# Two attention decodes on one core: moving the softmax steps of the sliding-window half, and loading the output weights in longer rows

## Chip, cores, metric

One core of one Trainium2 chip. The metric is device time of the core in microseconds; most executions of one kernel agree within 0.3%.

## The reference, cut

```python
# A: 4 batches, 32 query heads on 8 key heads, the last W = 2048 of 8192 keys
# B: 4 batches, 32 query heads on 32 key heads, all 8192 keys
q = (x @ wq).reshape(B, 1, 32, 128).transpose(0, 2, 1, 3)
scores = einsum("bhqd,bhkd->bhqk", q, k) * 128 ** -0.5
o = einsum("bhqk,bhkd->bhqd", softmax(scores), v)
out = o.transpose(...).reshape(B, 1, 4096) @ wo         # wo: 4096 x 512
# A's and B's results side by side, all tensors bf16
```

B's caches alone are 537 MB, A's part that is used 34 MB, the four weights 17 MB. Every byte is read once.

## The kernel before

The program works through chunks: 8 of A (one key head, all four batches: 2 MB of keys, 2 MB of values, 512 KB of output weights), then 64 of B (two heads of one batch: 4 MB of keys, 4 MB of values; every four chunks 256 KB of output weights). PE is TensorE, DVE VectorE, ACT ScalarE. One engine, SP (SyncE), issues all loads in order; each waits until PE has freed its buffer. PE transposes keys in groups of 8 tiles of 128, DVE or ACT copies each group out of PSUM (where PE's results land), PE makes scores from it two groups later. Values of chunk c-1 are multiplied between the keys of c and of c+1.

```python
def dma_wo(g):                              # A's output weights: 512 rows of 1 KB
    src = A_wo[g * 4 * P:(g + 1) * 4 * P, :].rearrange("(hl d) n -> d hl n", d=P)
    ... waits=[("fin", g - 2)] ...          # the slot is free when chunk g-2 has its output product

# in emit_T: who copies group g of transposed keys
if (g % 3 == 2) if c >= NCA else (g % 2 == 1):   # ACT, else DVE

def keys_part(c):
    for g in range(ch["NG"]):               # 8 groups in A, 16 in B
        emit_T(ch["s"] + g)
        if g >= SLAG: emit_S(ch["s"] + g - SLAG)
        if 1 <= c < NCA and g == 2: stats_gmax(c - 1)
        if 1 <= c < NCA and g == 3: stats_exp(c - 1)   # bias, shift, exponent, masked spread, sums
        if 2 <= c < NCA and g == 4: emit_fin(c - 2)    # output product
        if 1 <= c < NCA and g == 6: norm_sum(c - 1)
        ...

def values_part(c, nxt):                    # values of c, last scores of nxt
    todo = {2: lambda: emit_S(late[0]), 5: lambda: scores_last(nxt)}
    ...

# after the last pair of chunks
norm_sum(NC - 1)
for g in range(chunks[NC - 1]["NG"]): emit_pv(NC - 1, g)
pv_done(NC - 1); emit_fin(NC - 1)

# PE's instructions are written as two loops, over pairs of chunks of A and of B; the code
# between them (A's serial end) is straight. Both loop heads stand at slot 0 of a block of 256.
sch.emit_looped("pe", e, sems, loop_on(mybir.EngineType.PE, (0, 0)))
```

## Time and profile before

| | before |
|---|---|
| time, median of 3 runs | 1379.57 us (1378.76 to 1380.17) |
| span of the profiled run | 1378.8 us |
| DMA | 587.5 MB, 426 GB/s over the span, plateau 431 to 433 |
| PE busy | 86%, VectorE 47%, ScalarE 32% |

The page splits the span into 40 slices of 34.5 us. The kernel is bound by the DMA: the way to read it is to ask in which slices it moves less than the plateau, and what the issuing queue waited for there. The prediction shows those lines.

### The profile page before, as it was taken

How to read it: one execution, taken by the hardware profiler on the slowest of the kernel's cores; microseconds unless marked ns; L12 is line 12 of the kernel's file. 1: busy time of each engine (PE TensorE's matmuls, PEld its weight loads, DVE VectorE, ACT ScalarE, POOL GpSimd, SP SyncE). 2: the span in 40 equal slices, each digit the busy share in tenths (PEclk: the TensorE clock that was granted, in tenths of full speed). 3: DMA queues.
4: the chain of work that ended last, by engine and by line, in shares of the span. 5: the costliest groups of instructions: out<-in, count | busy, mean ns of one | idle time of the engine just before them, and what ended most of it. 6: DMA issues, size and time to landing. Idle time of an engine off the chain costs nothing.

```text
span 1378.8 us, 59410 instructions
## 1 busy us (share of the span) xinstructions
PE 1179.3 (86%) x26901; PEld 1134.8 (82%) x26901; DVE 641.3 (47%) x1337; ACT 436.0 (32%) x649; POOL 4.8 (0%) x18
## 2 busy tenths in 40 slices
PE   4888799898889888888898888888888898888988
PEld 4776799887879888888898788888888888888887
DVE  1664355454444444444454444444444444444443
ACT  1553234232323322323333223332332233223322
POOL 1000000000000000000000000000000000000000
PEclk9898999999999999999999999999999999999999
DMA  9999999999999999999999999999999999999998
GB/s 401 414 417 416 394 429 432 429 432 433 428 432 433 427 433 432 430 432 432 429 432 433 433 428 433 431 430 432 430 431 433 433 428 432 433 429 432 430 428 356
DMA packets 30373, 587.53 MB, mean 426 GB/s; under 512 B 2816, under 2 KB 11024, under 8 KB 11408
## 3 DMA queue, kind: packets, MB, share of 16 engines
q1 hardware_dynamic: 30328, 587.22, 99.7%
q8 instruction: 16, 0.26, 0.1%
q14 instruction: 5, 0.04, 0.0%
q10 hardware_dynamic: 24, 0.01, 0.0%
HBM read 587.21 MB, written 0.01 MB: 426 GB/s over the span
## 4 chain that ended last, share of the span: by engine, by line
DMA 58%; PE 37%; DVE 2%; issue 1%; SPq 1%; ACT 0%; DVEq 0%
DMA kv<-in_B_k_cache_dram 54%; PE tr L382 22%; PE sc L384 10%; PE po L384 3%; DMA kv<-in_B_v_cache_dram 2%; PE fin L384 2%; DMA kv<-in_B_wq_dram 2%; DVE sA L501 1%; PE ms L384 1%; SPq L339 1%; DVE kt L452 0%; DVE sA L499 0%; ACT pba L564 0%; PE ms L382 0%; DVE rm L510 0%
## 5 line engine op out<-in xcount | busy, mean ns | idle before, releaser
L382 PE MATMUL tr<-identb,kv 128*128 128x128 bf16 x8704 | 703.9, 232 | 155.4 <-DMA kv<-in_B_k_cache_dram 152.2
L452 DVE COPY kt<-tr 128x1024 bf16<-128x1024 bf16 x736 | 503.2, 691 | 466.6 <-PE tr L382 465.3
L382 PEld LDWEIGHTS tr<-identb,kv 128*128 128x128 bf16 x8704 | 559.4, 105 | 181.2 <-DMA kv<-in_B_k_cache_dram 97.0
L450 ACT ACTIVATE kt<-tr 128x1024 bf16<-128x1024 bf16 x352 | 360.0, 1023 | 625.9 <-PE tr L382 625.5
L384 PE MATMUL sc<-qb,kt 128*128 128x64 bf16 x8704 | 447.7, 196 | 9.8 <-DVE kt L452 9.5
L384 PEld LDWEIGHTS sc<-qb,kt 128*128 128x128 bf16 x8704 | 369.7, 100 | 13.8 <-DVE kt L452 11.1
L384 PE MATMUL po<-pbb,kv 128*128 128x64 bf16 x8320 | 294.5, 192 | 8.7 <-issue 6.8
L384 PEld LDWEIGHTS po<-pbb,kv 128*128 128x128 bf16 x8320 | 267.3, 97 | 11.0 <-issue 7.0
L549 ACT ACTIVATE pbb<-sc,negb 64x128 bf16<-64x128 f32 x128 | 51.0, 399 | 297.8 <-DVE negb L539 297.0
L515 DVE TENSOR_REDUCE rm<-sc 64x1 f32<-64x128 f32 x128 | 36.9, 289 | 95.0 <-PE sc L384 94.1
L527 DVE TENSOR_REDUCE gm<-ms 1x2 f32<-1x128 f32 (+1 forms) x72 | 20.1, 279 | 44.9 <-PE ms L382 44.8
L539 DVE COPY negb<-ms 128x1 f32<-128x1 f32 (+1 forms) x72 | 11.4, 158 | 57.1 <-PE ms L384 57.1
L384 PE MATMUL ms<-identf,gx 1*128 1x1 f32 (+1 forms) x144 | 27.8, 260 | 0.0
L384 PEld LDWEIGHTS ms<-identf,gx 1*128 1x128 f32 (+1 forms) x144 | 21.7, 188 | 4.9 <-issue 0.9
L549 ACT ACTIVATION_READ_ACCUMULATOR pbb<-sc,negb 64x1 f32 x128 | 23.7, 185 | 0.0
L382 PE MATMUL ms<-identf,rm 128*1 128x128 f32 (+1 forms) x72 | 19.7, 274 | 2.3 <-DVE rm L510 2.3
L384 PE MATMUL po<-pba,kv 128*128 128x64 bf16 x512 | 20.1, 199 | 0.5 <-ACT pba L564 0.5
L384 PE MATMUL fin<-wos,oz 128*4 128x512 bf16 x66 | 19.6, 378 | 0.3 <-DVE oz L629 0.3
L384 PEld LDWEIGHTS po<-pba,kv 128*128 128x128 bf16 x512 | 17.9, 102 | 0.6 <-ACT pba L564 0.6
L531 DVE TENSOR_SCALAR gx<-gm 1x128 f32<-1x128 f32 (+1 forms) x72 | 15.9, 221 | 2.7 <-DVE gm L527 0.2
L384 PE MATMUL ms<-xT,kv 128*128 128x4 bf16 x256 | 7.1, 166 | 9.1 <-DMA kv<-in_A_wq_dram 4.6
L384 PEld LDWEIGHTS ms<-xT,kv 128*128 128x128 bf16 x256 | 7.0, 104 | 9.3 <-DMA kv<-in_A_wq_dram 4.7
(46 smaller groups left out, 139.5 us busy)
## 6 DMA issues: line engine op xcount, KB each, us to landing
kv<-in_B_k_cache_dram SPq DMA_DIRECT2D x63, 4096.0 KB, 27.3
kv<-in_B_v_cache_dram SPq DMA_DIRECT2D x63, 4096.0 KB, 32.0
kv<-in_A_k_cache_dram SPq DMA_DIRECT2D x8, 2048.0 KB, 12.6
kv<-in_A_v_cache_dram SPq DMA_DIRECT2D x8, 2048.0 KB, 14.2
kv<-in_A_wq_dram SPq DMA_DIRECT2D x1, 4096.0 KB, 12.2
kv<-in_B_wq_dram SPq DMA_DIRECT2D x1, 4096.0 KB, 27.2
wor<-in_A_wo_dram SPq DMA_DIRECT2D x8, 512.0 KB, 8.5
wos<-in_B_wo_dram SPq DMA_DIRECT2D x16, 256.0 KB, 20.8
```

The source lines that it names most:

```text
L339: sch.add_dma("sp", lambda e, x=x: e.dma_start(dst[:, x], src[:, x]), "d_vl%d" % i, waits=waits, key=("vl", j0))
L382: sch.add("pe", lambda e: e.transpose(o, l, r), waits, key)
L384: sch.add("pe", lambda e: e.matmul(o, l, r, start=start, stop=stop), waits, key)
L450: sch.add("act", lambda e: e.activation(dst, src, ACTF.Copy), waits=waits, key=("ev", s))
L452: sch.add("dve", lambda e: e.tensor_copy(dst, src), waits=waits, key=("ev", s))
L501: emit = lambda e, src=src, b=b: e.scalar_tensor_tensor(out=t, in0=src, scalar=mk[:, b:b + 1], in1=t, op0=ALU.mult, op1=ALU.add)
L515: sch.add("dve", lambda e, src=src, pp=pp: e.tensor_reduce(out=rm[pp, m, 0:1], in_=src, axis=AX.X, op=ALU.max), waits=[("S", ch["s_last"]) ...
L527: sch.add("dve", lambda e: e.tensor_reduce(out=gm[0:C, m, 0:U], in_=src, axis=AX.X, op=ALU.max), waits=[("trm", c)], key=("gmax", c))
L531: sch.add("dve", lambda e: e.tensor_scalar(out=dst, in0=gv, scalar1=-scale, scalar2=None, op0=ALU.mult), waits=[("gmax", c)], key=("gx", c))
L539: sch.add("dve", lambda e: e.tensor_copy(negb[:, m, 0:C], ms[:, col:col + C]), waits=[("bc", c)], key=("negb", c))
L549: sch.add("act", lambda e, src=src, pp=pp, n=n, u=u: e.activation(pbv[pp, :, u], src, ACTF.Exp, bias=negb[pp, m, 0:1], scale=scale, accum_ ...
```

## The change

Its intent: in A, take the score work on DVE out of the way of the key copies, so that PE keeps up with the DMA; and load both output weights in rows of 4 KB (A) and 2 KB (B) instead of 1 KB. A longer row puts neighbouring weight rows on one partition, so the head outputs have to be permuted to match: small matmuls with 0/1 matrices ("selection") and copies. For the last chunk the weights are permuted instead (`emit_wol`).

```diff
-            src = A_wo[...].rearrange("(hl d) n -> d hl n", d=P)
+            src = A_wo[...].rearrange("(p r) n -> p (r n)", r=4)
-            src = B_wo[...].rearrange("(hl d) n -> d hl n", d=P)
+            src = B_wo[...].rearrange("(p r) n -> p (r n)", r=2)
-            if (g % 3 == 2) if c >= NCA else (g % 2 == 1):
+            if (g % 3 == 2) if c >= NCA else (g in (0, 1, 3, 5)):
+        def emit_sel(c):                    # 4 (A) or 2 (B) small matmuls, as many DVE copies
+            ...
+        def emit_wol():                     # 4 matmuls of 512 columns, one ACT and one DVE copy
+            ...
+        A_ORDER = {1: ['gmax-1'], 2: ['bc-1', 'shift-1'], 3: ['exp-1'], 5: ['sums-1', 'sel-2'],
+                   6: ['spread-1'], 7: ['norm-1', 'fin-2']}     # key group: step and chunk back
-            todo = {2: lambda: emit_S(late[0]), 5: lambda: scores_last(nxt)}
+            todo = {... the same for B ...} or {0: lambda: emit_S(late[0]), 1: lambda: scores_last(nxt)}   # A
+                if c >= NCA and c % 2 == 1 and g == 8:
+                    emit_sel(ahead(c, 2))
         norm_sum(NC - 1)
+        emit_wol()
         for g in range(chunks[NC - 1]["NG"]):
             emit_pv(NC - 1, g)
```

More of the change, by code (lines that the diff above doesn't have):

```diff
@@ L25 @@
 TRM0, BC0, L0, Q0, XT0 = 0, 256, 288, 320, 448
+Z0 = Q0
 class _Record:
@@ L240, in bass_concat_heads__sliding_block_cached__mha_block_cached__decode_kernel @@
         outsb = sb("outsb", [36, DO], BF16)
+        sel4 = sb("sel4", [P, 4, P], BF16)
+        sel2 = sb("sel2", [P, 2, P], BF16)
+        back2 = sb("back2", [P, 2, 2, P], BF16)
+        zA = sb("zA", [P, 2, 16], BF16)
+        zB = sb("zB", [P, 8], BF16)
+        wol = sb("wol", [P, 2, DO], BF16)
         tr = ps("tr", [P, NTRB, TG * P], BF16)
@@ L274, in bass_concat_heads__sliding_block_cached__mha_block_cached__decode_kernel @@
         sch.add("pool", lambda e: e.memset(pbt[1][:, :, :], 0.0), key=("c_pb", 1))
+        for r in range(4):
+            sch.add("pool", lambda e, r=r: e.affine_select(
+                out=sel4[:, r, :], in_=onesb[:, :], pattern=[[0, 4], [-4, 32]], compare_op=ALU.is_equal,
+                fill=0.0, base=-r, channel_multiplier=1), waits=["c_onesb"])
+        for r in range(2):
+            sch.add("pool", lambda e, r=r: e.affine_select(
+                out=sel2[:, r, :], in_=onesb[:, :], pattern=[[0, 2], [-2, 64]], compare_op=ALU.is_equal,
+                fill=0.0, base=-r, channel_multiplier=1))
+            for u in range(2):
+                sch.add("pool", lambda e, r=r, u=u: e.affine_select(
+                    out=back2[:, u, r, :], in_=onesb[:, :], pattern=[[1, P]], compare_op=ALU.is_equal,
+                    fill=0.0, base=P * u - r, channel_multiplier=-2), key="c_sel" if r == u == 1 else None)
         half_of = {}
@@ L304, in dma_wo @@
         def dma_wo(g):
-            src = A_wo[g * 4 * P:(g + 1) * 4 * P, :].rearrange("(hl d) n -> d hl n", d=P)
+            src = A_wo[g * 4 * P:(g + 1) * 4 * P, :].rearrange("(p r) n -> p (r n)", r=4)
             slot = wo_slot(g)
-            dst = wor[:, slot, :].rearrange("p (hl n) -> p hl n", hl=4)
+            dst = wor[:, slot, :]
             sch.add_dma("sp", lambda e: e.dma_start(dst, src), "d_wo%d" % slot,
@@ L311, in dma_wos @@
         def dma_wos(hp):
-            src = B_wo[2 * hp * P:2 * (hp + 1) * P, :].rearrange("(hl d) n -> d hl n", d=P)
-            sch.add_dma("sp", lambda e: e.dma_start(wos[:, :, :], src), "d_wos",
+            src = B_wo[2 * hp * P:2 * (hp + 1) * P, :].rearrange("(p r) n -> p (r n)", r=2)
+            sch.add_dma("sp", lambda e: e.dma_start(wos[:, :, :].rearrange("p r n -> p (r n)"), src), "d_wos",
                         waits=[("fin", NCA + 4 * hp - 1)] if hp else [], key=("wos", hp))
@@ L532, in stats_gmax, with stats_bc @@
                     waits=[("gmax", c)], key=("gx", c))
-        def stats_exp(c):
-            ch = chunks[c]
-            ab, m, C, U = ch["ab"], c % NSM, ch["C"], ch["U"]
+        def stats_bc(c):
+            m, C = c % NSM, chunks[c]["C"]
             col = BC0 + (c % 2) * 16
@@ L540, in stats_exp, with probs_of @@
             ms_read[:] = [("negb", c)]
-            i = c % NPB
-            prev = c - NPB
-            pw = [("c_pb", ab)] + ([("pv", prev)] if prev >= (0 if ab == 0 else NCA) else [("pv", NONE)] if prev == NCA - 1 else [])
-            pbv = pbt[ab][:, i, 0:ch["NT"] * ch["UC"]].rearrange("p (j x) -> p j x", x=ch["UC"])
-            if ab == 1:
-                for u, pp in HALVES:
-                    src = sc[pp, c % 2, 0:NTB * 2].rearrange("p (j u) -> p u j", u=2)[:, u, :]
-                    n = 2 * ((c - NCA) % 2) + u
-                    sch.add("act", lambda e, src=src, pp=pp, n=n, u=u: e.activation(
-                        pbv[pp, :, u], src, ACTF.Exp, bias=negb[pp, m, 0:1], scale=scale, accum_out=rst[1][pp, n:n + 1]),
-                        waits=[("negb", c), "c_rs"] + rs_read[NSM] + pw, key=("exp", c) if u == 1 else None)
-                sc_read[c % 2] = [("exp", c)]
-                sch.tk[("rs", c)] = sch.tk[("exp", c)]
-                return
+        def probs_of(c):
+            ch = chunks[c]
+            return pbt[ch["ab"]][:, c % NPB, 0:ch["NT"] * ch["UC"]].rearrange("p (j x) -> p j x", x=ch["UC"])
@@ new lines, in exp_B @@
+        def exp_B(c):
+            m, prev = c % NSM, c - NPB
+            pw = [("c_pb", 1)] + ([("pv", prev)] if prev >= NCA else [("pv", NONE)] if prev == NCA - 1 else [])
+            for u, pp in HALVES:
+                src = sc[pp, c % 2, 0:NTB * 2].rearrange("p (j u) -> p u j", u=2)[:, u, :]
+                n = 2 * ((c - NCA) % 2) + u
+                sch.add("act", lambda e, src=src, pp=pp, n=n, u=u: e.activation(
+                    probs_of(c)[pp, :, u], src, ACTF.Exp, bias=negb[pp, m, 0:1], scale=scale, accum_out=rst[1][pp, n:n + 1]),
+                    waits=[("negb", c), "c_rs"] + rs_read[NSM] + pw, key=("exp", c) if u == 1 else None)
+            sc_read[c % 2] = [("exp", c)]
+            sch.tk[("rs", c)] = sch.tk[("exp", c)]
@@ L555, in stats_exp, with shift_A, exp_A @@
+        def shift_A(c):
+            C = chunks[c]["C"]
             t = sA[:, c % 2, :].rearrange("p (j c) -> p j c", c=C)
-            bias = bcast(negb[:, m, 0:C], [[0, NTA], [1, C]])
+            bias = bcast(negb[:, c % NSM, 0:C], [[0, NTA], [1, C]])
             sch.add("dve", lambda e: e.scalar_tensor_tensor(out=t, in0=t, scalar=scale, in1=bias, op0=ALU.mult, op1=ALU.add),
                     waits=[("negb", c)], key=("shift", c))
-            ev = eA[:, c % 2, :]
-            sch.add("act", lambda e: e.activation(ev, sA[:, c % 2, :], ACTF.Exp),
+        def exp_A(c):
+            sch.add("act", lambda e: e.activation(eA[:, c % 2, :], sA[:, c % 2, :], ACTF.Exp),
@@ L562, in stats_exp, with spread_A @@
                     waits=[("shift", c)] + ([("exp", c - 2), ("rs4", c - 2)] if c >= 2 else []), key=("exp1", c))
-            for b in range(NB):
+        def spread_A(c, bs):
+            for b in bs:
                 sch.add("act", lambda e, b=b: e.activation(
-                    pbv.rearrange("p j (b c) -> p j b c", b=NB)[:, :, b, :], ev.rearrange("p (j c) -> p j c", c=C),
+                    probs_of(c).rearrange("p j (b c) -> p j b c", b=NB)[:, :, b, :], eA[:, c % 2, :].rearrange("p (j c) -> p j c", c=REP),
@@ L566, in stats_exp, with sums_A @@
                     ACTF.Copy, scale=mk[:, b:b + 1]),
-                    waits=[("exp1", c), "mk"] + pw if b == 0 else [], key=("exp", c) if b == NB - 1 else None)
-            sch.add("dve", lambda e: e.tensor_reduce(out=rs4[:, m, :], in_=ev.rearrange("p (j c) -> p c j", c=C), axis=AX.X, op=ALU.add),
+                    waits=[("exp1", c), "mk", ("c_pb", 0)] + ([("pv", c - NPB)] if c >= NPB else []) if b == 0 else [],
+                    key=("exp", c) if b == NB - 1 else None)
+        def sums_A(c):
+            m = c % NSM
+            sch.add("dve", lambda e: e.tensor_reduce(out=rs4[:, m, :], in_=eA[:, c % 2, :].rearrange("p (j c) -> p c j", c=REP), axis=AX.X, op=ALU.add),
@@ L569, in stats_exp @@
                     waits=[("exp1", c)], key=("rs4", c))
             sch.add("dve", lambda e: e.tensor_tensor(
-                out=rst[0][:, m, :].rearrange("p (b c) -> p b c", b=NB), in0=bcast(rs4[:, m, :], [[0, NB], [1, C]]),
-                in1=bcast(mk[:, :], [[1, NB], [0, C]]), op=ALU.mult),
+                out=rst[0][:, m, :].rearrange("p (b c) -> p b c", b=NB), in0=bcast(rs4[:, m, :], [[0, NB], [1, REP]]),
+                in1=bcast(mk[:, :], [[1, NB], [0, REP]]), op=ALU.mult),
                 waits=[("rs4", c)], key=("rs", c))
@@ L627, in norm_out @@
                 i1 = rz[:, :].rearrange("p (x y) -> p x y", x=2)
-            waits = [("rinv" if 0 <= c < NCA else "rz", c), ("pv", c)] + ([("fin", c - 2 if c != NCA + 1 else NONE)] if c >= 2 else [])
+            waits = [("rinv" if 0 <= c < NCA else "rz", c), ("pv", c)] + ([("sm", c - 2 if c != NCA + 1 else NONE)] if c >= 2 else [])
             sch.add("dve", lambda e: e.tensor_tensor(out=o, in0=i0, in1=i1, op=ALU.mult), waits=waits, key=("oT", c))
             po_read[:] = [("oT", c)]
+        def emit_sel(c):
+            if 0 <= c < NCA:
+                sel, x, n, z, k = sel4, oT[:, c % NSM, :], 16, zA[:, c % 2, :], 4
+                free = [("fin", c - 2)] if c >= 2 else []
+            else:
+                sel, x, n, z, k = sel2, oz[:, :], 8, zB[:, :], 2
+                free = [("fin", c - 2 if c - 2 >= NCA else NONE)] if c != NONE else []
+            for r in range(k):
+                pe_mm(ms[:, Z0 + r * n:Z0 + (r + 1) * n], sel[:, r, :], x,
+                      waits=[("oT", c)] + ms_read if r == 0 else [], key=("sm", c) if r == k - 1 else None)
+            for h in range(k):
+                pp = slice(h * P // k, (h + 1) * P // k)
+                src = ms[pp, Z0:Z0 + k * n].rearrange("p (r b h) -> p h r b", r=k, b=NB)[:, h]
+                sch.add("dve", lambda e, src=src, pp=pp: e.tensor_copy(z[pp, :].rearrange("p (r b) -> p r b", r=k), src),
+                        waits=[("sm", c)] + free if h == 0 else [], key=("z", c) if h == k - 1 else None)
+            ms_read[:] = [("z", c)]
+        def emit_wol():
+            for u in range(2):
+                o = tr[:, u, :].bitcast(F32)
+                for r in range(2):
+                    pe_mm(o, back2[:, u, r, :], wos[:, r, :], start=r == 0, stop=r == 1,
+                          waits=[("wos2", NC - 1)] if u == r == 0 else [], key=("back", u) if r else None)
+                if u == 0:
+                    sch.add("act", lambda e, o=o: e.activation(wol[:, 0, :], o, ACTF.Copy), waits=[("back", 0)], key=("wol", 0))
+                else:
+                    sch.add("dve", lambda e, o=o: e.tensor_copy(wol[:, 1, :], o), waits=[("back", 1)], key=("wol", 1))
         def emit_fin(c):
@@ L634, in emit_fin @@
             p0 = 0 if ab == 1 else 32
-            if ab == 1:
+            if c == NC - 1:
                 ov = oz[:, :].rearrange("p (b u) -> p b u", u=2)
-                ops = [(ov[:, :, u], wos[:, u, :]) for u in range(2)]
-                waits = [("oT", c), ("wos2", c)]
-            else:
-                w = wor[:, wo_slot(c), :].rearrange("p (hl n) -> p hl n", hl=4)
-                ov = oT[:, c % NSM, :].rearrange("p (u c) -> p u c", c=REP)
-                ops = [(ov[:, :, cc], w[:, cc, :]) for cc in range(REP)]
-                waits = [("oT", c), ("wo", c)]
+                ops = [(ov[:, :, u], wol[:, u, :]) for u in range(2)]
+                waits = [("oT", c), ("wol", 0), ("wol", 1)]
+            elif ab == 1:
+                ops = [(zB[:, r * NB:(r + 1) * NB], wos[:, r, :]) for r in range(2)]
+                waits = [("z", c), ("wos2", c)]
+            else:
+                w = wor[:, wo_slot(c), :].rearrange("p (r n) -> p r n", r=4)
+                ops = [(zA[:, c % 2, r * NB:(r + 1) * NB], w[:, r, :]) for r in range(4)]
+                waits = [("z", c), ("wo", c)]
             lastc = NC - 1 if ab == 1 else NCA - 1
@@ L657, in pv_done, with do_A @@
                 norm_out(c)
+        A_ORDER = {1: ['gmax-1'], 2: ['bc-1', 'shift-1'], 3: ['exp-1'], 5: ['sums-1', 'sel-2'], 6: ['spread-1'], 7: ['norm-1', 'fin-2']}
+        def do_A(what, c):
+            name, n = what.split("-")
+            c -= int(n)
+            if c < 0:
+                return
+            {"gmax": stats_gmax, "bc": stats_bc, "shift": shift_A, "exp": exp_A, "sums": sums_A, "norm": norm_sum,
+             "spread": lambda c: spread_A(c, range(4)), "spread01": lambda c: spread_A(c, (0, 1)), "spread23": lambda c: spread_A(c, (2, 3)),
+             "sel": emit_sel, "fin": emit_fin}[name](c)
         def keys_part(c):
@@ L666, in keys_part @@
                     emit_S(ch["s"] + g - SLAG)
-                if 1 <= c < NCA and g == 2:
-                    stats_gmax(c - 1)
-                if 1 <= c < NCA and g == 3:
-                    stats_exp(c - 1)
-                if 1 <= c < NCA and g == 6:
-                    norm_sum(c - 1)
-                if 2 <= c < NCA and g == 4:
-                    emit_fin(c - 2)
+                for what in A_ORDER.get(g, []) if c < NCA else []:
+                    do_A(what, c)
                 if c >= NCA and c % 2 == 0 and g == 6:
                     norm_sum(ahead(c, 1))
+                if c >= NCA and c % 2 == 1 and g == 8:
+                    emit_sel(ahead(c, 2))
                 if c >= NCA and c % 2 == 1 and g == 10:
@@ L684, in values_part @@
             late = list(range(ch["s_last"] + 1 - SLAG, ch["s_last"] + 1))
-            todo = {2: lambda: emit_S(late[0]), 5: lambda: scores_last(nxt)}
+            todo = {2: lambda: emit_S(late[0]), 5: lambda: scores_last(nxt)} if ch["ab"] == 1 else {0: lambda: emit_S(late[0]), 1: lambda: scores_last(nxt)}
             if ch["ab"] == 1:
                 todo[10] = lambda: stats_gmax(nxt)
-                todo[14] = lambda: stats_exp(nxt)
+                todo[14] = lambda: (stats_bc(nxt), exp_B(nxt))
             if nxt + 1 < NC:
@@ L707, in finish_A @@
         def finish_A():
-            stats_gmax(NCA - 1)
-            emit_fin(NCA - 2)
-            stats_exp(NCA - 1)
-            norm_sum(NCA - 1)
+            for what in ['gmax-1', 'sel-2', 'bc-1', 'shift-1', 'exp-1', 'spread-1', 'sums-1', 'fin-2', 'norm-1']:
+                do_A(what, NCA)
             for g in range(chunks[NCA - 1]["NG"]):
@@ L714, in finish_A @@
             pv_done(NCA - 1)
+            emit_sel(NCA - 1)
             emit_fin(NCA - 1)
@@ L726, in bass_concat_heads__sliding_block_cached__mha_block_cached__decode_kernel @@
                 emit_q(1)
-                pe_mm(fin[0:36, :], pbt[0][:, 1, 0:36], pbt[0][:, 1, 0:DO], stop=False, waits=[("c_pb", 1)])
+                pe_mm(fin[0:36, :], pbt[0][:, 1, 0:36], pbt[0][:, 1, 0:DO], stop=False, waits=["c_sel"])
             values_part(None if c == 0 else NONE if c == NCA else c - 1, c)
```

## The prediction

> **What bounds the kernel now.** I read the page first: slices, then the DMA issues. The kernel streams 587 MB of keys and values, and the share of the DMA engines stands at 9 tenths in all slices but the last.
>
> ```profile
> PEclk9898999999999999999999999999999999999999
> DMA  9999999999999999999999999999999999999998
> GB/s 401 414 417 416 394 429 432 429 432 433 428 432 433 427 433 432 430 432 432 429 432 433 433 428 433 431 430 432 430 431 433 433 428 432 433 429 432 430 428 356
> DMA packets 30373, 587.53 MB, mean 426 GB/s; under 512 B 2816, under 2 KB 11024, under 8 KB 11408
> ```
>
> The reader is to see three things: a plateau of 431 to 433; dips to 427-429 every two to three slices (one 256 KB load of B's output weights each time); and five poorer slices at the start, the sliding-window problem A, whose 8 chunks end near 131 us. Most of the 11024 packets under 2 KB are the 8192 rows of 1 KB of the two output weights.
>
> Next the windows, to see whether the DMA ever lacks work.
>
> ```profile
> 48.00:104.00 56.00, 48.86 (x955) 41.35 (x954) 34.10 (x87) 30.72 (x45) 0.00 (x0) 0.94 1.02 417
> 106.00:108.00 2.00, 0.96 (x18) 0.79 (x15) 1.89 (x7) 1.02 (x1) 0.00 (x0) 1.00 0.83 268
> 162.00:166.00 4.00, 3.40 (x97) 3.23 (x95) 1.78 (x3) 1.08 (x2) 0.00 (x0) 1.00 0.82 287
> 180.00:1360.00 1180.00, 1027.75 (x23764) 999.59 (x23762) 555.06 (x1130) 368.20 (x550) 0.00 (x0) 0.94 1.00 431
> ```
>
> Columns: stretch, length, busy time of PE, PEld, DVE, ACT, POOL, clock, DMA share, GB/s. In A the share is full at only 417 GB/s, so the packets are dear. There are two holes, at 107 and at 164 us. Counting in the trace's packet records how many packets are in flight (16 when full), they are worth 0.5 and 1.45 us. Why they open, the queue's issues show:
>
> ```profile
> 94.42 0.54 SPq L330 DMA_DIRECT2D kv<-in_A_v_cache_dram  x1
> 100.85 0.37 SPq L308 DMA_DIRECT2D wor<-in_A_wo_dram  x1
> 105.65 0.54 SPq L330 DMA_DIRECT2D kv<-in_A_v_cache_dram  x1
> ...
> 151.32 0.33 SPq L348 DMA_DIRECT2D kv<-in_B_v_cache_dram  x1
> 164.52 0.33 SPq L348 DMA_DIRECT2D kv<-in_B_k_cache_dram  x1
> ```
>
> A load goes out when PE has freed its buffer. PE's A chunks start their value products at 55.66, 68.22, 79.48, 92.07, 103.30 and 115.89 us (chain of waits): 12.05 us a chunk. The packets of successive A output-weight loads start at 47.79, 59.07, 70.30, 81.59 and 92.88 us: the DMA needs 11.27. PE loses 0.8 us a chunk on the DMA until the queue runs dry at 107 and, after A's serial end (118 to 131 us), at 164. Later PE has time to spare: it waits 152.2 us in all for B's keys, 56 times.
>
> Where PE loses time in A, the timeline of one chunk shows:
>
> ```profile
> 93.95 0.48 DVE L499 TENSOR_SCALAR sA<-sc,mk 128x256 f32<-128x256 f32 x1 [2.12 <-PE sc L384]
> 94.47 1.52 DVE L501 SCALAR_TENSOR_TENSOR sA<-sc,mk,sA 128x256 f32<-128x256 f32 x3
> 96.03 0.60 DVE L510 TENSOR_REDUCE rm<-sA 128x4 f32<-128x256 f32 x1
> 96.76 1.29 DVE L452 COPY kt<-tr 128x1024 bf16<-128x1024 bf16 x2
> 97.51 0.41 PE L384 MATMUL sc<-qb,kt 128*128 128x64 bf16 x8 [1.57 <-DVE kt L452]
> ```
>
> The first transposed keys of the next chunk wait behind 2.6 us of score work on DVE; PE stands 1.6 us.
>
> **The Trainium skill.** (1) "DMA: Bandwidth & Descriptors", section "Why small descriptors are slow": a fixed overhead per packet. The records agree: median 46 ns for 1 KB, 85 for 2 KB, 159.5 for 4 KB, 613 for 16 KB; the line through 1 and 4 KB leaves some 8 ns at zero size. (2) "TensorE: Matmul & The Clock Gate", "What's actually happening": half clock after an idle window of about 3.4 us. The trace has half-clock windows of 3413 ns, in A every 23.9 us; two of the listed chunks' 12.6 us against 11.25 come from there. (3) Same page, "Wait — 56ns, not 53.3ns?": 215.7 ns between 512-column matmuls at full clock. Four such take 1.03 us here with the last one's latency of 378 ns, so the starts are 0.22 apart.
>
> **The change part by part.**
>
> *Rows of A's output weights, 1 to 4 KB.* A chunk of the DMA now takes 11.28 us; its two 2 MB loads are 2 x 8 x 0.613 = 9.81, leaving 1.47 for 512 KB. New: 128 packets over 16 engines, 8 x 0.1595 = 1.28. Saved 0.19 x 8 = 1.5 us of DMA time.
>
> *Rows of B's, 1 to 2 KB.* Now 16 x 46 = 0.736 us a load (two neighbouring 4 MB loads are 0.74 us longer where one lies between them). New: 8 x 0.085 = 0.68. Saved 0.056 x 16 = 0.9 us.
>
> *Selection matmuls.* A row layout puts weight rows 4p..4p+3 on partition p, so the outputs must be permuted: 4 small matmuls and 4 DVE copies per A chunk, 2 and 2 per two B chunks. A: 4 x about 0.06 = 0.25 us of PE (L's pair of small ones occupies 0.11 to 0.24), 4 x 0.16 = 0.64 of DVE (16-column PSUM operations take 0.16). In B this lies inside PE's spare time.
>
> *Moved steps in A.* Key copies 0, 1, 3, 5 on ACT (was 1, 3, 5, 7); last scores after the first two value groups (was 3 and 6); softmax spread over groups 1 to 7. By hand at full clock, from a chunk's first value product: group spacings are 0.235 (values), 0.24 (scores), 0.45 (transposes). Last scores end at 0.95; DVE scores and row maximum 1.2 to 3.8; transposes 0 and 1 end at 3.3; ACT copies them 3.0 to 5.1, beside DVE, so the 1.6 us stand mostly goes. Row-maximum transpose 3.95, global maximum and its spread on DVE to 4.95, bias matmul 5.3, shift to 6.2, ACT copy 3 to 7.1, exponent to 7.5, DVE sums to 8.1, selection copies to 8.75, ACT copy 5 to 8.5, masked spread on ACT to 10.2, PE's last transposes, sum and output products to 10.3. Then the next values. So some 10.4 us against 11.25 now, and with the throttled windows about 11.1 against 12.05. Over seven chunks PE is some 6 us earlier at A's end. The serial end keeps its length: the output product moves out of the wait for the bias (it cost 1.8 us there), the selection adds about 1 us.
>
> The holes need PE to gain 0.5 + 1.45 plus the 1.5 us by which the DMA becomes faster, about 3.5 us. With 6 both close: 2.0 us saved.
>
> *End of the kernel.* Four 512-column matmuls restore the last weights' layout before the last value products, after the last sum. The last value group now starts at 1374.99 after 0.22 us of waiting for its load:
>
> ```profile
> 1370.85 0.39 PE L384 MATMUL ms<-rsb,onesf 128*128 128x4 f32 x2 [0.86 <-ACT pbb L549]
> 1371.09 3.67 PE L384 MATMUL po<-pbb,kv 128*128 128x64 bf16 x120
> 1374.99 0.41 PE L384 MATMUL po<-pbb,kv 128*128 128x64 bf16 x8 [0.22 <-DMA kv<-in_B_v_cache_dram]
> ```
>
> 4 x 0.215 = 0.86, less 0.22 of slack: +0.64 us on the path that sets the end. Copies of them on ACT and DVE hide under the values.
>
> *Sum:* -1.5 - 0.9 - 2.0 + 0.64 = -3.8 us, from 1379.57 to **1375.8**.
>
> **The rivals.** (a) *PE gains little in A* (masked spread late on ACT holds up the value products, or throttled windows lengthen). Then buffer release sets the DMA, the 1.5 us of A come back as longer holes, and only 0.9 - 0.64 stays: about 1379. For it: the spread ends within 0.1 us of need in my hand schedule. Against: each of DVE and ACT is busy only 7.2 and 6.2 of 11.23 us in a chunk. (b) *The output product, three groups later, delays the next weight load and the keys queued behind it, and opens a new hole.* For it: the queue waits in order, and loads were issued as little as 3.3 us ahead of their turn (100.85 against 104.17). Against: the key load behind it waits for the last transpose anyway, and a faster PE restores the lead. It would cost 1 to 3 us: 1377 to 1379. (c) *The small rows overlap with neighbours*: in A some 16.5 to 16.9 packets are in flight during 1 KB stretches, so their real cost could be under my 1.47; I used spacings, which include it. (d) *Wins of several per cent* are excluded: 579 MB in rows of 16 KB and more at their packet times are already 1338 us by the medians (2432 x 0.613 / 16 + 16384 x 1.216 / 16).
>
> **Range and chances.** The parts that only take DMA time (2.4 us) are safe if PE keeps up; the holes are the doubt. 8 in 10: 1373.0 to 1379.0. Two per cent is 27.6 us, several times everything here: faster 0.01, within 2% 0.98, slower 0.01.
>
> **What would show it.** Packets under 2 KB fall by 8192 to about 2830. The fifth slice rises from 394 towards 420, the windows at 107 and 164 us show a full DMA share, and A's slices go from 414-417 to above 420. Chunks of A come 11.1 us apart, and the wait of the scores for the DVE key copies (8.7 us in six waits) is mostly gone. At the end PE no longer waits for the last value load, and the last value group starts 0.6 us after it landed. Wrong if a hole stays in A, if PE's A chunks stay at 12 us, or if the tail after the last load grows by more than 1 us.

## The result

The changed kernel took 1379.55 us (median of 6 runs, 1377.74 to 1380.56); the kernel before took 1379.78 us (6 runs, 1377.29 to 1381.94) beside it. The ratio is 0.9998, 95% interval 0.9985 to 1.0011. Ratios here are the mean time of one kernel's runs over that of the other's of the same rounds, so not quite the ratio of the medians quoted. The forecast of 1375.8 (1373.0 to 1379.0) was wrong: nothing was gained.

The page of the changed kernel, slices and queues:

```profile
PEclk9897999999999999999999999999999999999998
GB/s 400 424 424 432 384 430 436 426 438 429 431 433 427 433 431 435 429 432 433 428 433 434 427 437 429 433 429 432 435 429 435 427 433 432 430 434 430 434 424 318
DMA packets 25254, 587.55 MB, mean 426 GB/s; under 512 B 2816, under 2 KB 2832, under 8 KB 6288
q8 instruction: 17, 0.28, 0.1%
```

The small packets fell by 8192 as foretold, and A's slices 2 to 4 rose from 414-417 to 424-432. But the fifth slice fell, from 394 to 384, and the last from 356 to 318. So the DMA was faster where it was meant to be, and lost it in two places. One more 16 KB instruction packet than before (there 16) looks like nothing; it turned out to be the clue.

Windows of the changed kernel (columns as in the prediction: clock, DMA share and GB/s come last):

```profile
48.00:104.00 56.00, 51.05 (x1081) 45.08 (x1082) 41.44 (x120) 31.64 (x48) 0.00 (x0) 1.00 1.01 425
106.00:108.00 2.00, 2.00 (x30) 1.27 (x28) 1.77 (x5) 1.67 (x5) 0.00 (x0) 1.00 0.99 420
140.00:144.00 4.00, 3.16 (x95) 3.06 (x93) 1.15 (x2) 1.02 (x1) 0.00 (x0) 1.00 0.71 238
161.00:165.00 4.00, 3.41 (x104) 3.29 (x101) 1.43 (x3) 1.02 (x1) 0.00 (x0) 1.00 0.89 324
1361.00:1368.00 7.00, 6.06 (x113) 5.99 (x114) 0.66 (x3) 0.00 (x0) 0.00 (x0) 0.51 0.98 414
```

The hole at 107 us is closed. Another opened at 140, one at 161-165 stayed. And near the end PE was granted half its clock for 7 us ("half clock" from here on; the trace's clock records say 1361.1 to 1367.9).

The moved steps worked. The timeline of a chunk of A, answering the one in the prediction:

```profile
97.92 0.48 DVE L523 TENSOR_SCALAR sA<-sc,mk 128x256 f32<-128x256 f32 x1 [1.10 <-PE sc L408]
98.44 1.52 DVE L525 SCALAR_TENSOR_TENSOR sA<-sc,mk,sA 128x256 f32<-128x256 f32 x3
100.58 0.62 PE L406 MATMUL tr<-identb,kv 128*128 128x128 bf16 x8 [1.28 <-DMA kv<-in_A_k_cache_dram]
```

PE now waits 1.28 us for keys from the DMA, not for DVE. The value products of A's chunks start at 55.36, 66.03, 76.58, 86.46, 96.81 and 107.80 us: 10.49 us a chunk, 12.05 before. B's first value load went out at 120.27 us, 9.4 us earlier than before (129.71). But the key load after it went out only 1.0 us earlier (first line before, second changed):

```profile
142.16 0.33 SPq L348 DMA_DIRECT2D kv<-in_B_k_cache_dram  x1
141.12 0.33 SPq L372 DMA_DIRECT2D kv<-in_B_k_cache_dram  x1
```

The 8.4 us in between are lost on PE, most of them in one gap at the end of A (first line before, where no gap stands; then changed):

```profile
131.33 1.51 PE L382 MATMUL tr<-identb,kv 128*128 128x128 bf16 x24
121.66 1.87 PE L408 MATMUL fin<-wor,zA 128*4 128x512 bf16 x4 [0.81 <-DVE zA L681]
128.97 2.74 PE L406 MATMUL tr<-identb,kv 128*128 128x128 bf16 x24 [5.43 <-issue]
```

"issue" says that the engine waited for nothing that the profile shows. B's first keys landed at 123.28 us by the trace's records, so for 5.7 us before PE starts they are not what it waits for. In the trace's records of PE's queue one instruction spans the gap: the branch into B's loop, at 121.8 us, took 6.83 us. In the kernel before it took 0.30. Counting PE's instructions from A's loop head to this branch gives 827 + 180 = 1007 before and 859 + 196 = 1055 after. A's loop head is at slot 0 of a block of 256, so four blocks hold 1024: the changed code runs 31 over into a fifth, and B's loop, pinned to slot 0, moves one block further on. The Trainium skill, "Runtime: NRT & Kernel Launch", section "Instruction fetch mechanics", says that blocks of 256 instructions are fetched in sequence and that a taken branch whose target is outside the window forces a fetch of the target before execution goes on. The trace has the packet: 16 KB on the instruction queue from 126.14 to 127.25 us, 1.7 us before PE starts. All five profiles with a late branch (table below) have 17 such packets, all seven others 16.

The end of the changed kernel, PE:

```profile
1361.94 1.46 PE L408 MATMUL po<-pbb,kv 128*128 128x64 bf16 x24 [3.07 <-DMA kv<-in_B_v_cache_dram]
1370.39 0.38 PE L408 MATMUL ms<-rsb,onesf 128*128 128x4 f32 x2 [0.85 <-ACT pbb L575]
1370.85 0.81 PE L408 MATMUL tr<-wos,back 128*128 128x512 bf16 x3
1371.50 3.91 PE L408 MATMUL po<-pbb,kv 128*128 128x64 bf16 x128
```

The same place before:

```profile
1365.07 0.88 PE L384 MATMUL po<-pbb,kv 128*128 128x64 bf16 x24 [1.71 <-DMA kv<-in_B_v_cache_dram]
```

24 value matmuls take 1.46 us where they took 0.88 before. Before, PE waited 0.22 us for the last load; now all has landed (last load packet at 1371.35 us) and PE still has 4 us to go. From the first line of the changed kernel to the end of the last value product it is 13.5 us; before, from 1365.07 to 1375.40, 10.3.

The two profiled spans are equal (1378.8 us), so what the loads gained, the tail lost: the last load packet ends at 1374.47 us before and 1371.35 after, 3.1 us sooner; from there to the end of the span it is 4.3 us before and 7.45 after, 3.1 us longer.

### The profile page after: what moved, and what is told of

Same layout as the page of the kernel before. It is cut to its first block, busy times and chain, and to the rows that moved or that the text cites. A ratio compares the mean times of both kernels' runs of the same rounds, so it can differ in the third digit from the quotient of the medians.

```text
span 1378.8 us, 59836 instructions
## 1 busy us (share of the span) xinstructions
PE 1179.7 (86%) x27000; PEld 1137.7 (83%) x27001; DVE 656.7 (48%) x1434; ACT 434.8 (32%) x650; POOL 7.3 (1%) x28
## 4 chain that ended last, share of the span: by engine, by line
DMA 61%; PE 36%; DVE 1%; issue 1%; ACT 0%; SPq 0%; DVEq 0%; ACTq 0%
DMA kv<-in_B_k_cache_dram 56%; PE tr L406 22%; PE sc L408 9%; PE po L408 2%; DMA kv<-in_B_v_cache_dram 2%; DMA kv<-in_B_wq_dram 2%; PE fin L408 2%; DMA kv<-in_A_k_cache_dram 1%; PE ms L408 1%; DVE sA L525 1%; ACT pba L595 0%; DVE rm L534 0%; DVE sA L523 0%; PE ms L406 0%; DVE zA L681 0%
## 5 line engine op out<-in xcount | busy, mean ns | idle before, releaser
L408 PE MATMUL fin<-wos,zB 128*4 128x512 bf16 x64 | 19.0, 378 | 0.0
L681 DVE CAST zB<-ms 64x8 bf16<-64x8 f32 x64 | 10.5, 163 | 8.9 <-PE ms L408 8.5
```

Source lines behind the costliest of these rows:

```text
L408: sch.add("pe", lambda e: e.matmul(o, l, r, start=start, stop=stop), waits, key)
L681: sch.add("dve", lambda e, src=src, pp=pp: e.tensor_copy(z[pp, :].rearrange("p (r b) -> p r b", r=k), src), waits=[("sm", c)] + free if h ...
```

## Experiments

Theory: (i) the branch into B's loop waits for a fetch since the code grew past 1024 instructions, and this keeps the holes open; (ii) at the end, half clock after PE's 3 us of waiting and the layout matmuls put PE, not the DMA, on the path. Rivals: the 5.4 us have another cause (keys, clock); the longer rows or the new order bring nothing anyway; the selection work slows PE.

All runs gave a correct result. "Branch" is the branch into B's loop; "holes" the DMA time missing from 16 packets in flight, summed over the 5 us stretches between 10 and 1300 us that lack more than 0.15; "tail" is from the last load packet to the end of the span. These three are from each run's profile, out of the trace's records, which no view prints.

| run | median us (runs) | ratio, 95% interval | branch | holes | last load | tail |
|---|---|---|---|---|---|---|
| before | 1379.78 (6) | 1 | 0.30 | 2.2 | 1374.5 | 4.3 |
| changed | 1379.55 (6) | 0.9998 (0.9985-1.0011) | 6.83 | 2.5 | 1371.4 | 7.45 |
| changed, again | 1380.03 (5) | 1.0000 (0.9987-1.0014) | 6.91 | 4.3 | 1373.5 | 7.4 |
| loop at slot 64 | 1375.08 (5) | 0.9972 (0.9958-0.9985) | 0.18 | 0 | 1368.5 | 4.8 |
| before, branch made late | 1382.91 (5) | 1.0022 (1.0009-1.0036) | 6.30 | 6.1 | 1377.5 | 4.3 |
| layout before the sum | 1376.97 (5) | 0.9987 (0.9973-1.0001) | 5.83 | 1.4 | 1370.4 | 4.3 |
| dummies only | 1378.84 (6) | 0.9992 (0.9978-1.0005) | 7.15 | 3.3 | 1373.4 | 4.8 |
| slot 64, layout | 1375.28 (5) | 0.9968 (0.9955-0.9982) | 0.29 | 1.3 | 1369.4 | 6.5 |
| slot 64, layout, dummies | 1374.53 (5) | 0.9964 (0.9951-0.9978) | 0.29 | 0 | 1368.9 | 4.3 |
| order alone | 1378.38 (5) | 0.9992 (0.9979-1.0006) | 0.30 | 0 | 1371.6 | 5.1 |
| rows alone | 1394.09 (4) | 1.0108 (1.0092-1.0123) | 0.30 | 16.1 | 1387.4 | 4.8 |
| rows alone, spaced | 1383.66 (6) | 1.0032 (1.0019-1.0045) | 0.30 | 6.7 | 1377.2 | 4.8 |

### 1. B's loop at slot 64

```diff
-            sch.emit_looped("pe", e, sems, loop_on(mybir.EngineType.PE, (0, 0)))
+            sch.emit_looped("pe", e, sems, loop_on(mybir.EngineType.PE, (0, 64)))
```

> The changed kernel, only with PE's loop of problem B placed 64 instruction slots into a block of 256 (was 0), so that PE runs into it without skipping to the next block. My theory: in the changed kernel the branch into B's loop (6.8 us in the trace, PE idle 5.43 us before B's first transposes) waits for a block of instructions, because A's loop and serial end grew from 1007 to 1055 instructions, over 4 blocks of 256. Then this run has no such idle time (under 1 us), B's first transposes start near 123.5 instead of 128.97 us, the DMA holes at 140-143 and 161-165 us (2.1 us) are gone, and the DMA ends 2 us earlier; the time falls by 0 to 2 us only, as the tail stays PE's. Rival: the 5.4 us are a wait for B's first keys or a clock effect; then the idle time and the holes stay as they are.

Measured: 1375.08 us. PE at the end of A, then the two windows of the holes:

```profile
121.67 1.02 PE L408 MATMUL fin<-wor,zA 128*4 128x512 bf16 x4 [0.81 <-DVE zA L681]
123.41 1.51 PE L406 MATMUL tr<-identb,kv 128*128 128x128 bf16 x24 [0.71 <-DVE outsb L716]
```

```profile
140.00:144.00 4.00, 3.01 (x47) 2.88 (x47) 0.65 (x3) 0.05 (x1) 0.00 (x0) 0.67 1.03 442
161.00:165.00 4.00, 2.41 (x67) 2.33 (x67) 0.68 (x4) 0.00 (x0) 0.00 (x0) 1.00 1.00 426
```

B's first transposes start at 123.41, 5.6 us sooner, just after B's first keys landed (123.29), and both holes are closed. The key load that went out at 141.12 in the changed kernel goes out at 134.41. One number in the source, with no arithmetic or wait changed, is worth about 4 us (4.5 between the medians, 3.6 between the ratios, whose intervals meet only at 0.9985); I had expected 0 to 2, as I took the half clock at the end for a fixture. Its profile has none there (PE waited 1.58 us), so the tail is 4.8 us.

### 2. The same miss brought into the kernel before

```diff
-            sch.emit_looped("pe", e, sems, loop_on(mybir.EngineType.PE, (0, 0)))
+            sch.emit_looped("pe", e, sems, loop_on(mybir.EngineType.PE, (48, 0)))
```

> The kernel before, only with PE's loop of problem A moved 48 slots into its block, so that its 1007 instructions end as far past a block boundary (31) as in the changed kernel; B's loop stays at slot 0 of the next block. My theory: the branch into B's loop now takes 5 to 7 us instead of 0.30, B's first transposes start 5 us later (131.3 to 136), and the DMA hole at 164 us grows from 1.45 to 5-7 us: slower by 3 to 5 us. Rival (the wait has another cause than the block boundary): nothing changes, branch 0.3 us, time within 1 us.

Measured: 1382.91 us, 3.0 us slower by the ratio. Its timeline:

```profile
129.03 1.38 PE L384 MATMUL fin<-wor,oT 128*4 128x512 bf16 x4 [0.34 <-DVE oT L629]
135.80 2.42 PE L382 MATMUL tr<-identb,kv 128*128 128x128 bf16 x21 [5.39 <-issue]
```

The same 5.4 us appear in a kernel that has none of the change, with as many instructions past the boundary. The holes grow from 2.2 to 6.1 us. This and run 1 settle (i): the position of the code causes the wait, and the wait makes the holes.

### 3. The layout matmuls before the last sum

```diff
-        norm_sum(NC - 1)
         emit_wol()
+        norm_sum(NC - 1)
```

> The changed kernel, only with the four layout matmuls of the end put before the last sum (where PE waits 0.85 us for the exponent) instead of after it. My theory: the path after the exponent is 0.65 us shorter: from the first value product of the last-but-one chunk to the last value product's end 0.65 us less at the same clock; time 0.5-0.8 us less, hard to see in the timing alone. Rival (the copies of the layout matmuls or the last load hold up the end): no change in that stretch.

Measured: 1376.97 us; the interval of its ratio overlaps the changed kernel's, so the times alone don't tell the two apart. The end of its PE:

```profile
1366.78 0.39 PE L408 MATMUL ms<-rsb,onesf 128*128 128x4 f32 x2
1367.02 3.69 PE L408 MATMUL po<-pbb,kv 128*128 128x64 bf16 x120
1370.89 0.41 PE L408 MATMUL po<-pbb,kv 128*128 128x64 bf16 x8 [0.18 <-DMA kv<-in_B_v_cache_dram]
```

The wait for the exponent is now filled (none is shown before the sum, 0.85 us before), the values follow the sum at once, and PE again waits for the last load. The tail is 4.3 us, as before the change; with the layout matmuls after the sum and full clock it is 4.8 (run 1). So they cost 0.5 us. The rest of the median's gain over the changed kernel is not theirs: this profile has no half clock at its end although PE waited 3.05 us there (experiment 5 says why), and smaller holes.

### 4. Both repairs, and PE kept busy

```diff
+            if c is not None and c >= NCA and nxt % 2:
+                for _ in range(12):
+                    pe_mm(po[:, 128:512], identb[:, :], pbt[0][:, 0, 0:384])
             for g in range(16):
```

with the edits of 1 and 3. (`nxt` is odd for every second B chunk; the last-but-one values are among those that get the dummies.)

> Both repairs together, and 12 dummy matmuls of 384 columns (about 2 us) ahead of the value products of every odd B chunk, which write PSUM columns nobody reads: they keep PE at work while it waits for the last-but-one values, so that the clock is not halved there (in the changed kernel it was half from 1361.1 to 1367.9 us and cost 2.7 us on the path that sets the end). My theory: the tail runs at full clock, the stretch from the landing of the last-but-one values to the end of the last value product is about 10.3 us instead of 13.5, the DMA has no holes after 10 us, and the time is 4 to 5.5 us under the changed kernel: 1374 to 1375.5. Rival (the dummies take PE time that B needs, or the tail's half clock is not what costs): time as the changed kernel or slower, PE's waits for B's keys gone.

Measured: 1374.53 us, 1374.32 to 1375.06, the fastest and tightest of all. The dummies, the values after them, and the window:

```profile
1356.29 2.12 PE L408 MATMUL po<-pba,identb 128*128 128x384 bf16 x12
1359.51 0.88 PE L408 MATMUL po<-pbb,kv 128*128 128x64 bf16 x24 [1.11 <-DMA kv<-in_B_v_cache_dram]
```

```profile
1355.00:1369.00 14.00, 12.83 (x319) 11.05 (x316) 3.46 (x10) 2.53 (x6) 0.00 (x0) 1.00 0.83 344
```

PE's idle time ahead of the values is 1.1 us and the clock stays at 1.00 (third last column); from the first of these values to the end of the last it is 10.3 us. As expected.

### 5. How often does half clock strike the end?

Three runs ask this: the changed kernel again, the two repairs without dummies, and the changed kernel with dummies alone.

> The changed kernel once more, for a second profile and more times. The branch into B's loop should take 5.5 to 7 us again and the DMA holes be 1.5 to 2.5 us. Where PE's half clock falls is open: if the profile has it away from the last 20 us, the span should be 1376 to 1377 and the last value product end about 3.5 us after the last load; if it falls there again, 1378 to 1379 and the stretch from the last-but-one values' landing to the last value product's end is 13 us instead of 11.

> The changed kernel with B's loop at slot 64 and the layout matmuls before the last sum, without the dummy matmuls. If the half clock at the end strikes only some executions, this run is at 1374.5 to 1375 in most of them with one or two 1 to 2.5 us longer; if the dummies were what made the tight run at 1374.5, this one is at 1375 or above throughout. Without the layout matmuls after the sum it should be 0.5 us under the run with the slot alone.

> The changed kernel with nothing repaired, only the 12 dummy matmuls ahead of the value products of odd B chunks. My theory: the branch still takes 5.5 to 7 us and the holes stay at 2 to 4 us, but the end runs at full clock: span less last load packet 4.8 us instead of 7.4, the time 1376 to 1378 and never above 1379. Rival (half clock at the end is no cost of the changed kernel's usual execution): median 1379.5 as the changed kernel.

The changed kernel again had half clock from 1363.2 us for 6.8 us, after a wait of 3.04 us, tail 7.4; its holes (4.3 us) and its span (1380.9 us) lie above the 2.5 and 1379 that I had expected. The two repairs without dummies (median 1375.28) had it in the profiled execution, from 1358.8 us, after this wait:

```profile
1359.98 1.46 PE L408 MATMUL po<-pbb,kv 128*128 128x64 bf16 x24 [3.22 <-DMA kv<-in_B_v_cache_dram]
```

That execution, which also had 1.3 us of holes, took 1377.6 us; the other four of the same kernel took 1374.38 to 1375.66. I had expected most at 1374.5 to 1375 and a median 0.5 us under run 1; it is 0.2 above. With dummies nothing of five runs was above 1375.06. So half clock at the end comes in some profiled executions and not in others, and costs 2.2 us there (tail 6.5 against 4.3 us); neither profile with dummies has it. That it also makes the spread of the runs without a trace is argued, not shown. The dummies alone brought the tail back to 4.8 us as expected, but the median to 1378.84 only, and two of six runs were above 1379 (1379.41 and 1380.04); I had expected 1376 to 1378 and never above 1379. Without the branch repaired, that kernel's holes were 3.3 us. So the branch is the larger part. What the clock is worth shows in the tails; in the times the dummies' ratio (0.9992) is not clear of the changed kernel's (0.9998).

The traces say when half clock comes. Its records change only on a grid of 3413 ns. Count PE's idle time in each grid window after 20 us, in all twelve traces (from the packed records, which no view prints; PE's ends are modelled): each of the 415 full-clock windows with over 2.0 us idle was followed by a half-clock one, none of the 3544 with under 1.5 us was, and of the 176 between them 61 were. So what counted is not how long a wait lasts but how much of it falls into one window. At the end, the waits of 3.04, 3.07 and 3.22 us put 2.15, 2.20 and 2.04 us into one; run 3's wait of 3.05 us fell across a boundary, 1.88 and 1.17 us, and had no half clock. The 1.1 us of wait that the dummies leave can't reach 1.5 by themselves.

### 6. Order alone and rows alone

Order alone: the old row layouts, no selection, no layout matmuls (the 0/1 matrices are still made on GpSimd at the start, and unused), loop at slot 64. Rows alone: old `todo`, old key copies, softmax steps at their old groups; first with selection and output product both at group 4, then with the product at group 6:

```diff
-        A_ORDER = {1: ['gmax-1'], 2: ['bc-1', 'shift-1'], 3: ['exp-1'], 5: ['sums-1', 'sel-2'], 6: ['spread-1'], 7: ['norm-1', 'fin-2']}
+        A_ORDER = {2: ['gmax-1'], 3: ['bc-1', 'shift-1', 'exp-1', 'spread-1', 'sums-1'], 4: ['sel-2', 'fin-2'], 6: ['norm-1']}
+        # spaced: 4: ['sel-2'], 6: ['norm-1', 'fin-2']
```

> One part of the change alone: the moved softmax steps, last scores and key copies of problem A, with the old 1 KB rows of both output weights, no selection matmuls and no layout matmuls at the end; B's loop at slot 64, so that it cannot skip a block. My theory: PE's A chunks become DMA-bound (11.3 us, was 12.05), the DMA holes at 107 and 164 us (2 us) go, the rows keep their cost (11.28 us a DMA chunk, 0.74 us a B load): 2 us under the kernel before, about 1377.7. Rival (the whole gain of the repaired kernel comes from the rows): as before, 1379.5.

> The other part alone: 4 and 2 KB rows with selection and layout matmuls, with the old places of the softmax steps and the old key copies in A; B's loop at slot 64. My theory: PE's A chunks take 12.1 to 12.5 us as before or more, so the 1.5 to 1.9 us that the DMA saves in A come back as larger holes (3.5 us or more in place of 2), B's loads save 1 us and the layout matmuls cost 0.65 at the end: within 1 us of the kernel before, 1378.5 to 1380. Rival (rows and order add up independently): 2 us under before, 1377.5.

> The rows alone again, because in the run with rows alone PE waited 2.2 us a chunk between the selection matmuls and the output product, which I had put back to back. Here the output product comes two key groups later, as in the change; softmax steps and key copies stay in their old places; B's loop at slot 64. My theory: those 2.2 us go, PE's A chunks take 12.0 to 12.5 us, still more than the DMA's 11.0, so the holes in A's time and after stay at 3 us or more and the time is 1378.5 to 1381. Rival (rows pay by themselves): 1377.5 or less, holes under 1.5 us.

Order alone: 1378.38 us, 1.1 us under the kernel before by the ratio (2 were expected; the interval includes 1), no holes, last load 2.9 us sooner; its profile had a 3.4 us half-clock stretch from 1361.4 us in the tail. It needs 841 + 180 = 1021 instructions to the branch: by this count the new order by itself would just have fitted (not run at slot 0).

Rows alone: 1394.09, far outside what I expected. The waits of its A stretch (44 to 118 us; total, times, longest) have a new line that neither kernel has, and the second version has the old one again, larger than before (8.7 in six waits):

```profile
PE fin L408 <- DVE zA L681: 11.2, 5, 2.3
```

```profile
PE sc L408 <- DVE kt L476: 11.1, 12, 1.7
```

Back to back, the output product waits 2.2 us a chunk for the copies of its own selection, which stand behind the sums on DVE. My version made that wait; it is no verdict on the rows. Spaced, it is 1383.66 us: value products start at 56.63, 68.77, 81.01, 93.16 and 105.36 us, 12.2 apart, so PE falls behind the faster DMA (11.05) and the holes grow to 6.7 us; chunks and holes as expected, the time above the expected 1378.5 to 1381. The rows without the order are a loss in both versions tried; with it (run 1) the last load comes 5.9 us sooner than before, of which the order alone gives 2.9.

## Why the prediction was wrong, point by point

- *Rows.* Right, a little small. A's weight loads start 11.05 us apart (47.41, 58.47, 69.50, 80.57, 91.63), 0.22 less, times 8 is 1.8 us (foretold 1.5). B's loads 78.380 apart instead of 78.458, times 16 is 1.2 us (foretold 0.9).
- *Moved steps.* Right, and by more than foretold. By hand 10.4 us a chunk came out at full clock, and 11.1 with half-clock windows; measured are 10.49, because from 48 to 104 us no half-clock window is left (clock 1.00, before 0.94). That part was not foreseen: of the 1.56 us gained a chunk, 0.8 (12.05 less 11.25) goes with the clock. PE is 9.4 us ahead at the first value load of B, where 6 were foretold.
- *Holes: the step that failed.* "With 6 both close: 2.0 us saved" took it that PE's lead at A's end reaches B's first key group. It did not: 6.83 us of branch ate it. The holes went from 2.2 to 2.5 us (4.3 in the second profile), where none were foretold. The prediction counted what the selection matmuls cost on PE and DVE, and not that they are instructions in a loop that had 17 to spare. No rival named this.
- *End: mis-sized.* Foretold +0.64 us; the layout matmuls measured 0.5, but the tail grew by 3.1 in the profiled run, because a DMA that runs ahead, a 3.07 us wait and 6.8 us of half clock fell together. That is the prediction's own sign of being wrong, a tail that grows by more than 1 us. It cited the clock rule for A and did not apply it to the wait at the end. Nor had it read the rule off the trace: in A the windows ahead of the half ones had 1.7 of 3.41 us idle, not a whole idle window.
- *The sum.* Foretold: rows -2.4, holes -2.0, end +0.64. In the profiled pair: rows -3.0, holes +0.3, tail +3.1, together +0.4 where the spans differ by 0.0.
- With the branch repaired (run 1), 1375.08 us lies 0.7 from the forecast of 1375.8, and for the reasons counted: rows -3.0, holes -2.2, tail +0.5.
- *Rival (a)* (PE gains little) and *(b)* (output product later delays loads) did not occur; (a) does occur with the rows alone.
- Two slips that change nothing: three of the five listed chunks, not two, take 12.6 us, and the loads of rival (d) are 577 MB, not 579.

What stays open: how many executions of the changed kernel end at half clock (two of two profiles did; other executions have no trace), how the last 2 of the 4 us between the changed kernel and run 1 split between holes and clock, and why PE waits 3.0 to 3.2 us for the last-but-one values in some profiles and 1.58 in run 1's.

## What to carry to other kernels

When instructions are added to a looped program, count them up to the next taken branch: 32 more in A's loop and 16 in its serial end turned a 0.3 us branch into one of 6.8, and one loop position undid it. When a wait that set the end is shortened, look at what the engine behind it does next, and at the clock it will do it with: the traces here give half clock after a 3.41 us window with more than some 2 us idle, so shorter waits can cost too. Before a gain is called absent, see where the last load ends: here it came 3.1 us sooner, and PE gave all of it back.

## What the Trainium skill lacked or had wrong

- "Runtime: NRT & Kernel Launch", "Instruction fetch mechanics", gives no duration for a branch out of the window. Here, with all 16 DMA engines busy, the branch into B's loop took 5.8 to 7.2 us in five profiles, 0.2 to 0.3 in the other seven. The same section gives PE room for 2048 instructions in one place and calls the store two lines of 16 KB in another. B's loop of 1607 instructions, over six blocks, turned some 30 times with no packet on the 16 KB instruction queue from 172 us to 1374 us. The larger figure fits, the smaller does not.
- "TensorE: Matmul & The Clock Gate", "HAM oscillation — how this bites in real kernels", states the rule as no PE idle gaps above about 3.4 us. Here gaps of 3.04, 3.07 and 3.22 us were followed by 6.8 us at half clock, and one of 3.05 was not. What decided in these traces was the idle time within one window of 3413 ns: over 2.0 us always (415 windows), under 1.5 us never (3544).
